# One decode step of two attention and SwiGLU layers: q in wider slices, accumulators opened by one matmul, x added by five matmuls

## The chip, the cores and the metric

The kernel runs on one core of one Trainium2 chip. The metric is device time in microseconds (us). Before the change the median of three runs is 528.95 us (528.78 to 529.55).

A core has five engines that run beside each other: TensorE (PE, with its weight loads listed apart as PEld), VectorE (DVE), ScalarE (ACT), GpSimd (POOL) and SyncE (SP). Sixteen DMA engines move data between HBM and the on-chip memory (SBUF); matmuls write to PSUM.

## The reference

One token `x` of 640 numbers goes twice through attention and a gated feed-forward net, with the same weights and the same cache both times:

```
x = x + A(layernorm(x));  x = x + B(layernorm(x));  x = x + A(layernorm(x));  x = x + B(layernorm(x))

A(x): q = x @ wq            # wq [640, 32*192]
      k, v = the last W = 4096 rows of each of 32 heads' caches, [4096, 192] each
      p = softmax(q k^T / sqrt(192));   return concat(p v) @ wo      # wo [32*192, 640]
B(x): return (silu(x @ w1) * (x @ w3)) @ w2     # w1, w3 [640, 1536], w2 [1536, 640]
```

All is bf16. Each head's k and v window is 1.5 MB, so one pass over wq, all k, all v, wo, w1, w3 and w2 is some 120 MB; what the second layer can reuse is limited by what fits into SBUF.

## The kernel before

**Pages.** `arena` is an SBUF tile of 16 slots (`NSLOT`), each of 6144 bf16 columns by 128 partitions (1.5 MB). Everything big arrives as a page of this size: five pages of wq (`("q", layer, c)`), one k and one v page per head, wo in pages `("o", layer, 0..4)` of nine chunks each (a chunk is 128 rows of wo, 640 columns), and w1, w3, w2 as `fa`, `fb`, `fc`, `fd`. The list `loads` (L158 to L191) holds all transfers in their order. `refill` (L193) issues the next one on SP's queue as soon as a slot is free; `done(key)` frees a slot after its last use. So transfers are in program order on one queue, and an issue waits for the instruction that last read the slot. Thirteen k pages of layer 0 stay in their slots for layer 1 (`RETAIN`; a fourteenth, `STASH`, is kept in PSUM and a side tile), which leaves about three slots free around the change of layers.

Two small tiles are loaded once, in layer 0, and used in both layers: `wo5`, the last three chunks of wo in layer 0's order, and `keep`, the last three chunks of w2. The heads are taken in groups of eight, in the order `ORDER = ((3, 2, 1, 0), (1, 0, 2, 3))`. The three chunks that wo5 holds come from group 0, the last of layer 0; in layer 1 the same tile is multiplied where the last three chunks of group 3 stand.

**The stages of a layer.** `layernorm` (L222) makes `xs`. `qproj` (L247) multiplies x with the five wq pages: per page 16 matmuls of 384 columns, four side by side in the PE array (`tile_position=(0, 32 * j)`), into one PSUM tile `q_ps`; ACT copies it to SBUF (L260), twelve small matmuls turn it (L262 to L267), DVE copies the turned q to `qt_sb` (L268). `build_w` (L270) places q of four heads as weights `wst` for the scores. Then `attention` runs over the heads: DVE transposes each k page (L293), PE multiplies it (`s_ps`), softmax follows in blocks of four heads, and the v pages are multiplied six heads later (`o_ps`). `combine` writes the result as columns of `otd`.

`wo_proj` (L392) multiplies otd with wo. Each product has one row, so four are set side by side in rows 0, 32, 64 and 96 of the accumulators `y_ps`, one for each half of the 640 columns. `y_open` (L383) first opens these accumulators: it multiplies a tile of zeros (`zero`, 128 x 32) with 320 columns, four times per accumulator, so that all rows hold 0. `y_to_residual` sums the four rows and adds them to the residual x, which stays in fp32 in `xsq[:, 0:5]`.

`ffn` (L412) multiplies with w1 and w3 (`g_ps`, `u_ps`), turns both with six small matmuls, and forms `htd` on ACT and DVE (L440 to L449). In layer 0 the product with w2 goes through y_open and y_to_residual as above. In layer 1 `last_rows` (L466) forms the output: four zero matmuls open `f_ps`, 20 fp32 matmuls add x (one column of xsq as weights, 32 columns of the 128 x 128 identity `ident` as data), and 48 products with w2 follow; DVE copies the rows (L482) and SP writes them out (L484). POOL builds `ident` in a free slot at the start of layer 1's ffn (L417, L418).

All engine instructions keep the order in which the code records them (`pin`). Every matmul is recorded in the helper `mm`, so the profile puts all of them on L80 and they are told apart by the tiles they write.

Of the kernel before, what the change touches and what calls it, by code (L numbers as in the profile page):

```python
# [41 lines left out]
def _ap(t, p0, npart, off, dims):  # L42
    ps = t.ap[0][0]
    return bass.AP(t.tensor, t.offset + p0 * ps + off, [[ps, npart]] + [list(d) for d in dims])
# [3 lines left out]
def kernel(  # L48
# [26 lines left out]
    def pin(ins):  # L75
        tc.keep_in_program_order(ins)
        return ins

    def mm(*a, **k):
        return pin(nc.tensor.matmul(*a, **k))  # L80
# [17 lines left out]
    nc.gpsimd.memset(sel4[:], 0.0)  # L98
    nc.gpsimd.affine_select(out=sel4[:], in_=sel4[:], compare_op=ALU.not_equal, fill=1.0, base=0,
                            pattern=[[-32, 4]], channel_multiplier=1)  # L100
    sel16 = cst.tile([P, 4, 4], BF16, name="sel16")
    nc.gpsimd.memset(sel16[:], 0.0)
    nc.gpsimd.affine_select(out=sel16[:], in_=sel16[:], compare_op=ALU.not_equal, fill=1.0, base=0,
                            pattern=[[-32, 4], [-1, 4]], channel_multiplier=1)


    sel = cst.tile([P, 2, HB, 16], BF16, name="sel")
# [20 lines left out]
    ptm = cst.tile([P, 16 * PW], BF16, name="ptm")  # L128
    otd = cst.tile([P, 48], BF16, name="otd")
    htd = cst.tile([P, 12], BF16, name="htd")  # L130
    zero = cst.tile([P, 32], BF16, name="zero")
    nc.gpsimd.memset(zero[:], 0.0)
    w20 = cst.tile([P, 768], BF16, name="w20")
    qt_sb = cst.tile([P, 2, 6, 16], BF16, name="qt_sb")
    rl = cst.tile([P, 1], F32, name="rl")


# [17 lines left out]
    def head(layer, g):  # L155
        return HG * ORDER[layer][g // HG] + g % HG

    for layer in range(2):  # L158
        for c in range(NCH):
            loads.append((("q", layer, c), [(0, PGW, wq_v[c])]))  # L160
        for i in range(H + LEAD):
            for kind, g, cache in (("v", i - LEAD, A_v_cache), ("k", i, A_k_cache)):
                if not 0 <= g < H:
                    continue
                h = head(layer, g)
                if kind == "k" and layer == 1 and h in RETAIN:
                    if h == STASH:
                        loads.append((("k", 1, h), []))
                    continue
                loads.append(((kind, layer, h),  # L170
                              [(0, PGW, cache[0, h, S0:SK, :].rearrange("(p t) d -> p (t d)", p=P))]))
        for w in range(6):
            parts, ci, end = [], 9 * w, min(9 * w + 9, 48)
            while ci < end:
                to = min(end, ci - ci % 12 + 12)
                parts.append((640 * (ci - 9 * w), 640 * (to - ci),
                              wo_v[ORDER[layer][ci // 12]][:, 640 * (ci % 12):640 * (ci % 12 + to - ci)]))
                ci = to
            if w < 5:
                loads.append((("o", layer, w), parts))  # L180
            elif layer == 0:
                assert len(parts) == 1 and parts[0][1] == 1920
                loads.append((None, [(wo5[:], parts[0][2])]))
        loads.append((("fa", layer), [(0, PGW, w1_v[:, 0:PGW])]))
        loads.append((("fb", layer), [(0, PGW, w3_v[:, 0:PGW])]))
        loads.append((("fc", layer), [(0, 1536, w1_v[:, PGW:]), (1536, 1536, w3_v[:, PGW:]),
                                      (3072, 2560, w2_v[:, 0:2560])]))
        fd = [(0, 3200)] if layer == 0 else [(0, 1280), (1280, 1280), (2560, 640)]
        loads.append((("fd", layer), [(o, n, w2_v[:, 2560 + o:2560 + o + n]) for o, n in fd]))
        if layer == 0:  # L190
            loads.append((None, [(keep[:], w2_v[:, 5760:7680])]))  # L191
# [55 lines left out]
    def qproj(layer):  # L247
        q_ps = ps_a.tile([P, 512], F32, tag="a", name="q_ps")
        for c in range(NCH):
            pg = page(("q", layer, c))  # L250
            for c2 in range(4):
                for j in range(4):
                    hp = 4 * j + c2
                    mm(q_ps[32 * j:32 * j + 32, 0:384], lhsT=xs[:, c, 3 - c2:35 - c2],
                       rhs=pg[:, 384 * hp:384 * hp + 384],
                       start=(c == 0 and c2 == 0), stop=(c == NCH - 1 and c2 == 3),
                       tile_position=(0, 32 * j))
            done(("q", layer, c))
        q_sb = w20
        pin(nc.scalar.copy(out=q_sb[:, 0:384], in_=q_ps[:, 0:384]))  # L260
        qt_ps = m_ps[0:32].rearrange("p (h i c) -> p h i c", h=2, i=6)
        for hh in range(2):  # L262
            for it in range(6):
                be, par = divmod(it, 2)
                o = 64 * (3 * hh + be) + par
                mm(qt_ps[:, hh, it, :], lhsT=q_sb[:, o:o + 63:2],
                   rhs=sel16[:].rearrange("p j c -> p (j c)"), start=True, stop=True)  # L267
        pin(nc.vector.tensor_copy(out=qt_sb[0:32], in_=qt_ps[:]))  # L268

    def build_w(b, first):  # L270
        engs = (nc.gpsimd, nc.scalar) + ((nc.vector, nc.vector) if first else (nc.gpsimd, nc.scalar))
        for a in range(4):
            dst = _ap(wst[:], 32 * a, 32, 8 * a + HB - 1, [[382, HB // 2], [191, 2], [32, 6]])
            src = _ap(qt_sb[:], 0 if first else 32 * a, 32, HB // 2 * b, [[1, HB // 2], [96, 2], [16, 6]])
            pin((engs[a].copy if engs[a] is nc.scalar else engs[a].tensor_copy)(out=dst, in_=src))  # L275
        if first:
            for a in range(1, 4):
                pin(nc.vector.tensor_copy(out=qt_sb[32 * a:32 * a + 32], in_=qt_sb[0:32]))
# [104 lines left out]
    def y_open(name):  # L383

        y_ps = [ps_a.tile([P, 512], F32, tag="a", name=f"{name}{i}") for i in range(2)]
        for nh in range(2):
            for j in range(4):
                mm(y_ps[nh][32 * j:32 * j + 32, 0:320], lhsT=zero[:], rhs=ptm[:, 0:320],
                   start=True, stop=False, tile_position=(0, 32 * j))
        return y_ps  # L390

    def wo_proj(layer):  # L392
        y_ps = y_open("y_ps")
        for w in range(6):
            pg = page(("o", layer, w)) if w < 5 else wo5
            for cc in range(min(9, 48 - 9 * w)):
                ci = 9 * w + cc
                j = ci % 4
                for nh in range(2):
                    mm(y_ps[nh][32 * j:32 * j + 1, 0:320], lhsT=otd[:, ci:ci + 1],  # L400
                       rhs=pg[:, 640 * cc + 320 * nh:640 * cc + 320 * nh + 320],
                       start=False, stop=(ci >= 44), tile_position=(0, 32 * j))
            if w < 5:
                done(("o", layer, w))
        y_to_residual(y_ps)
# [6 lines left out]
    def ffn(layer):  # L412
        if layer == 1:
            assert not loads
            spare = free[0] * PGW
            ident = arena[:, spare:spare + 256].bitcast(F32)
            nc.gpsimd.memset(ident, 0.0)  # L417
            nc.gpsimd.affine_select(out=ident, in_=ident, compare_op=ALU.not_equal, fill=1.0, base=0,  # L418
                                    pattern=[[-1, P]], channel_multiplier=1)
        g_ps = ps_a.tile([P, 512], F32, tag="a", name="g_ps")  # L420
        u_ps = ps_a.tile([P, 512], F32, tag="a", name="u_ps")
        for ps, kind, c0, c1, off in ((g_ps, "fa", 0, 4, 0), (u_ps, "fb", 0, 4, 0),
# [42 lines left out]

    def last_rows(ident):  # L466
        f_ps = ps_a.tile([P, 512], F32, tag="a", name="f_ps")
        for j in range(4):
            mm(f_ps[32 * j:32 * j + 32, 0:160], lhsT=zero[:], rhs=ptm[:, 0:160], start=True, stop=False,
               tile_position=(0, 32 * j))  # L470
        for c in range(NCH):
            for j in range(4):
                mm(f_ps[32 * j:32 * j + 1, c:160:NCH], lhsT=xsq[:, c:c + 1], rhs=ident[:, 32 * j:32 * j + 32],
                   start=False, stop=False, tile_position=(0, 32 * j))
        for fcx in (0, 1, 2, 3, 9, 10, 11, 4, 5, 6, 7, 8):
            pg, off = w2_chunk(1, fcx)
            for j in range(4):
                mm(f_ps[32 * j:32 * j + 1, 0:160], lhsT=htd[:, fcx:fcx + 1],
                   rhs=pg[:, off + 160 * j:off + 160 * j + 160],
                   start=False, stop=(fcx == 8), tile_position=(0, 32 * j))  # L480
        row = w20[:, 0:160]
        pin(nc.vector.tensor_copy(out=row, in_=f_ps[:, 0:160]))  # L482
        ps = row.ap[0][0]
        nc.sync.dma_start(out=out[0, 0, :].rearrange("(j i) -> j i", j=4),  # L484
                          in_=bass.AP(row.tensor, row.offset, [[32 * ps, 4], [1, 160]]))
# [69 lines left out]
```

## Time and profile before

| what | value |
| --- | --- |
| median of 3 runs | 528.95 us (528.78 to 529.55) |
| the profiled execution | span 527.8 us; its time around the span is not listed apart |
| read from HBM | 221.58 MB, 420 GB/s over the span |
| PE matmuls | 2487 in 275.8 us (52%) |
| PE weight loads | 2487 in 113.9 us (22%) |
| DVE | 393 instructions in 256.5 us (49%) |
| ACT | 192 in 62.3 us (12%) |
| POOL | 66 in 14.3 us (3%) |
| mean granted TensorE clock | 0.716 |

The span runs from the first to the last instruction of the program. A busy share is an average over stages with different limits, so a stage is read from its own window. "Idle before, <-releaser" is the time that an engine had nothing to do before an instruction, and what ended it. The granted clock is the share of TensorE's clock that it was given. An fp32 matmul shows as two weight loads and two matmuls in the trace, called passes here.

### The profile page before, as it was taken

The page shows a single profiled execution, that of the slowest core. Times are in us where ns is not written, and L with a number is a line of the kernel's source. Part 1 is how long each engine was busy: PE and PEld are TensorE (multiplying, and loading weights), DVE is VectorE, ACT ScalarE, POOL GpSimd, SP SyncE. Part 2 cuts the span into 40 slices and gives each one's busy share as a digit, 9 for nine tenths or more (in the row PEclk, how much of TensorE's full clock was granted, in tenths as well). Part 3 has the DMA queues.
Part 4 walks back from the last instruction along what each step waited for, and adds up shares of the span by engine and source line. Part 5 has one row for each costly group of instructions (what it writes and reads, how often), then busy time and mean ns, then how long its engine had stood idle before and what let it go on. Part 6 is the DMA issues. An engine that isn't in the chain of part 4 may idle for free.

```text
span 527.8 us, 6132 instructions
## 1 busy us (share of the span) xinstructions
PE 275.8 (52%) x2487; PEld 113.9 (22%) x2487; DVE 256.5 (49%) x393; ACT 62.3 (12%) x192; POOL 14.3 (3%) x66
## 2 busy tenths in 40 slices
PE   2354644463645555455445446678254655446545
PEld 1111212121212221122112212233121322112212
DVE  1199676656656475754001139431475654753001
ACT  1002020111102020102000002022111120202000
POOL 4000000000000000000000000000000000000000
PEclk9997968676766776586556557888677886586556
DMA  8999999999999999999999999999999999999995
GB/s 350 430 429 429 428 431 429 427 431 429 427 431 431 430 425 432 430 426 425 416 433 422 430 430 401 431 431 427 430 429 427 429 430 431 430 428 428 424 432 215
DMA packets 22356, 221.97 MB, mean 421 GB/s; under 512 B 2617, under 2 KB 2745, under 8 KB 5177
## 3 DMA queue, kind: packets, MB, share of 16 engines
q1 hardware_dynamic: 22184, 221.59, 99.1%
q8 instruction: 19, 0.31, 0.2%
q14 instruction: 9, 0.07, 0.0%
q10 hardware_dynamic: 144, 0.00, 0.0%
HBM read 221.58 MB, written 0.00 MB: 420 GB/s over the span
## 4 chain that ended last, share of the span: by engine, by line
DMA 86%; PE 6%; DVE 5%; ACT 1%; issue 1%; SPq 0%; DVEq 0%; ACTq 0%
DMA arena<-in_A_k_cache_dram 54%; DMA arena<-in_A_v_cache_dram 14%; DMA arena<-in_A_wo_dram 8%; DMA arena<-in_A_wq_dram 6%; DMA arena<-in_B_w_dram 5%; DVE arena L293 4%; PE s_ps L80 3%; PE o_ps L80 2%; PE y_ps L80 1%; SPq L203 0%; ACT w L330 0%; PE pss L80 0%; PE q_ps L80 0%; DVE t L315 0%; PE g_ps L80 0%
## 5 line engine op out<-in xcount | busy, mean ns | idle before, releaser
L80 PE MATMUL s_ps<-arena,wst 128*32 128x512 bf16 x768 | 155.2, 518 | 172.7 <-DVE arena L293 86.4
L293 DVE STREAM_TRANSPOSE arena<-arena 128x1536 uint32<-128x1536 uint32 x100 | 171.2, 1754 | 77.3 <-DMA arena<-in_A_k_cache_dram 77.0
L80 PE MATMUL o_ps<-arena,ptm 128*8 128x384 bf16 (+1 forms) x1024 | 116.7, 425 | 11.4 <-DMA arena<-in_A_v_cache_dram 11.3
L80 PEld LDWEIGHTS <-wst 128*32 128x32 bf16 x768 | 52.9, 115 | 257.9 <-issue 226.7
L80 PEld LDWEIGHTS <-ptm 128*8 128x8 bf16 (+1 forms) x1024 | 41.0, 100 | 49.0 <-issue 38.8
L325 ACT ACTIVATE tb<-m 32x16 f32<-32x16 f32 x16 | 3.4, 215 | 280.6 <-DVE m L322 280.6
L343 ACT COPY ptm<-w 32x64 bf16<-32x64 bf16 x80 | 23.6, 295 | 44.5 <-PE o_ps L80 41.4
L80 PE MATMUL y_ps<-arena,otd 128*1 128x320 bf16 x180 | 16.5, 448 | 15.0 <-DMA arena<-in_A_wo_dram 15.0
L80 PE MATMUL q_ps<-arena,xs 128*32 128x384 bf16 x160 | 14.5, 519 | 17.5 <-DMA arena<-in_A_wq_dram 14.9
L376 DVE SCALAR_TENSOR_TENSOR w<-pss,rl,mask 64x192 bf16<-64x192 f32 x16 | 6.7, 416 | 31.7 <-PE pss L80 31.7
L275 POOL COPY wst<-qt_sb 32x24 bf16<-32x24 bf16 x30 | 8.4, 281 | 434.4 <-PE s_ps L80 315.8
L333 DVE STREAM_TRANSPOSE w<-w 64x512 bf16<-64x512 bf16 x16 | 11.3, 705 | 14.4 <-ACT w L330 14.4
L241 DVE CAST w<-y_ps 128x320 bf16<-128x320 f32 x3 | 1.5, 492 | 33.8 <-PE y_ps L80 33.8
L315 DVE TENSOR_REDUCE t<-s_ps 64x1 f32<-64x512 f32 x16 | 10.6, 663 | 12.2 <-PE s_ps L80 12.1
L80 PEld LDWEIGHTS <-xs 128*32 128x32 bf16 x240 | 8.8, 125 | 35.1 <-issue 23.0
L268 DVE CAST qt_sb<-pss 32x192 bf16<-32x192 f32 x2 | 0.7, 345 | 30.9 <-PE pss L80 30.9
L343 DVE COPY ptm<-w 32x64 bf16<-32x64 bf16 x48 | 10.0, 208 | 11.7 <-PE o_ps L80 10.4
L348 DVE RECIPROCAL rl<-pss 64x1 f32<-64x1 f32 x16 | 2.6, 165 | 20.5 <-PE pss L80 20.4
L80 PEld LDWEIGHTS <-otd 128*1 128x1 bf16 x192 | 6.4, 102 | 25.2 <-issue 21.1
L330 ACT ACTIVATE w<-s_ps,nbt 64x512 bf16<-64x512 f32 x16 | 10.9, 682 | 5.6 <-DVE nbt L327 5.6
L369 ACT CAST w<-o_ps 128x384 bf16<-128x384 f32 x16 | 7.7, 478 | 31.7 <-PE o_ps L80 23.3
L80 PE MATMUL pss<-w,sel 128*64 128x192 bf16 x32 | 6.0, 273 | 9.5 <-ACT w L369 6.4
(81 smaller groups left out, 107.8 us busy)
## 6 DMA issues: line engine op xcount, KB each, us to landing
arena<-in_A_v_cache_dram SPq DMA_DIRECT2D x64, 1536.0 KB, 29.2
arena<-in_A_k_cache_dram SPq DMA_DIRECT2D x50, 1536.0 KB, 29.2
arena<-in_A_wq_dram SPq DMA_DIRECT2D x10, 1536.0 KB, 9.5
arena<-in_A_wo_dram SPq DMA_DIRECT2D x6, 1440.0 KB, 20.8
arena<-in_B_w_dram SPq DMA_DIRECT2D x4, 1536.0 KB, 10.9
arena<-in_A_wo_dram SPq DMA_DIRECT2D x4, 960.0 KB, 16.5
arena<-in_A_wo_dram SPq DMA_DIRECT2D x4, 480.0 KB, 15.0
arena<-in_B_w_dram SPq DMA_DIRECT2D x4, 384.0 KB, 14.8
```

The source lines that it names most:

```text
L80: return pin(nc.tensor.matmul(*a, **k))
L241: pin(nc.vector.tensor_copy(out=y_sb[:, 320:640], in_=y_ps[1][:, 0:320]))
L275: pin((engs[a].copy if engs[a] is nc.scalar else engs[a].tensor_copy)(out=dst, in_=src))
L293: pin(nc.vector.transpose(x[:, w * sp:w * (sp + 1)].bitcast(U32), x[:, w * sp:w * (sp + 1)].bitcast(U32)))
L315: pin(nc.vector.reduce_max(out=t0[:, 0:1], in_=s_ps[0:64, :], axis=AX.X))
L325: pin(nc.scalar.mul(out=tb[32:64, :].rearrange("p (a z) -> p a z", a=4)[:, :, 0:HB], in_=mb, mul=-SCALE))
L330: pin(nc.scalar.activation(out=e[:], in_=s_ps[0:64, :], func=ACTF.Exp, bias=nbt[:, 0:1], scale=SCALE, accum_out=l[:]))
L333: pin(nc.vector.transpose(et[:], e[:]))
L343: pin((eng.copy if eng is nc.scalar else eng.tensor_copy)(out=dst, in_=src))
L348: pin(nc.vector.reciprocal(out=rl[half], in_=rl_ps[half]))
L369: pin(nc.scalar.copy(out=o_sb[:, 0:384], in_=o_ps[:, 0:384]))
L376: pin(nc.vector.scalar_tensor_tensor(out=om, in0=ot_ps[half], scalar=rl[half], in1=mask[half].unsqueeze(2).broadcast_to([64, 16, 12]), op0 ...
```

## The change

Four edits are made together.

- **q.** wq's 6144 columns are taken as 12 slices of 512 instead of 16 of 384. A page now takes 12 matmuls, three after each other in each of the four column groups. The turn takes 16 matmuls of 12 columns instead of 12 of 16, and writes PSUM with a step of 16 elements; `qt_sb` now has one row of six per head, and build_w reads it contiguously.
- **Opening.** `zero` is one column, broadcast to 128, and one matmul opens a whole accumulator; y_open issues two instead of eight.
- **Kept chunks.** `wo_order` puts the three chunks of group 3 last in both layers, so wo5 holds what both layers multiply last. In layer 0 this changes the order in which wo's chunks are loaded and multiplied; in layer 1 the order stays.
- **x in the last product.** f_ps is not opened by zeros. POOL builds an identity of 32 columns repeated over four groups of partitions (`ident`, now a pair) and `xw`, 640 fp32 columns in which each group of 32 partitions holds x in one column per chunk. Five fp32 matmuls with 128 columns of xw as weights add x to all four rows at once, and the first of them opens f_ps.

```
-    zero = cst.tile([P, 32], BF16, name="zero")
+    zero = cst.tile([P, 1], BF16, name="zero")
...
+    def wo_order(layer):
+        last = ORDER[1][3]
+        kept = [12 * ORDER[layer].index(last) + e for e in (9, 10, 11)]
+        return [ci for ci in range(48) if ci not in kept] + kept
...
-            for c2 in range(4):
+            for c2 in range(3):
                 for j in range(4):
-                    hp = 4 * j + c2
-                    mm(q_ps[32 * j:32 * j + 32, 0:384], lhsT=xs[:, c, 3 - c2:35 - c2],
-                       rhs=pg[:, 384 * hp:384 * hp + 384],
+                    sl = 3 * j + c2
+                    mm(q_ps[32 * j:32 * j + 32, 0:512], lhsT=xs[:, c, 3 - c2:35 - c2],
+                       rhs=pg[:, 512 * sl:512 * sl + 512],
...
-        pin(nc.scalar.copy(out=q_sb[:, 0:384], in_=q_ps[:, 0:384]))
-        qt_ps = m_ps[0:32].rearrange("p (h i c) -> p h i c", h=2, i=6)
-        for hh in range(2):
-            for it in range(6):
-                be, par = divmod(it, 2)
-                o = 64 * (3 * hh + be) + par
-                mm(qt_ps[:, hh, it, :], lhsT=q_sb[:, o:o + 63:2],
-                   rhs=sel16[:].rearrange("p j c -> p (j c)"), start=True, stop=True)
+        pin(nc.scalar.copy(out=q_sb[:, 0:512], in_=q_ps[:, 0:512]))
+        qt_ps = m_ps[0:32].rearrange("p (s n) -> p s n", s=12)
+        for blk in range(8):
+            for par in range(2):
+                o = 64 * blk + par
+                mm(qt_ps[:, :, 2 * blk + par], lhsT=q_sb[:, o:o + 63:2],
+                   rhs=sel12[:].rearrange("p j c -> p (j c)"), start=True, stop=True)
...
         for nh in range(2):
-            for j in range(4):
-                mm(y_ps[nh][32 * j:32 * j + 32, 0:320], lhsT=zero[:], rhs=ptm[:, 0:320],
-                   start=True, stop=False, tile_position=(0, 32 * j))
+            mm(y_ps[nh][:, 0:320], lhsT=zero[:].broadcast_to([P, P]), rhs=ptm[:, 0:320], start=True, stop=False)
...
-            ident = arena[:, spare:spare + 256].bitcast(F32)
+            ident = arena[:, spare:spare + 64].bitcast(F32)
             nc.gpsimd.memset(ident, 0.0)
-            nc.gpsimd.affine_select(out=ident, in_=ident, compare_op=ALU.not_equal, fill=1.0, base=0,
-                                    pattern=[[-1, P]], channel_multiplier=1)
+            for j in range(4):
+                nc.gpsimd.affine_select(out=ident, in_=ident, compare_op=ALU.not_equal, fill=1.0, base=-32 * j,
+                                        pattern=[[-1, 32]], channel_multiplier=1)
+            xw = arena[:, spare + 64:spare + 64 + 1280].bitcast(F32)
+            nc.gpsimd.memset(xw, 0.0)
+            for j in range(4):
+                nc.gpsimd.tensor_copy(out=xw[32 * j:32 * j + 32, 32 * j:640:128], in_=xsq[32 * j:32 * j + 32, 0:NCH])
+            ident = (ident, xw)
...
-        for j in range(4):
-            mm(f_ps[32 * j:32 * j + 32, 0:160], lhsT=zero[:], rhs=ptm[:, 0:160], start=True, stop=False,
-               tile_position=(0, 32 * j))
+        eye, xw = ident
         for c in range(NCH):
-            for j in range(4):
-                mm(f_ps[32 * j:32 * j + 1, c:160:NCH], lhsT=xsq[:, c:c + 1], rhs=ident[:, 32 * j:32 * j + 32],
-                   start=False, stop=False, tile_position=(0, 32 * j))
+            mm(f_ps[:, c:160:NCH], lhsT=xw[:, 128 * c:128 * c + 128], rhs=eye, start=(c == 0), stop=False)
```

## The prediction

> **What bounds the kernel now.** I read the page first, then the chain, then the stages by window, and last the timeline of the closing microseconds.
>
> ```profile
> span 527.8 us, 6132 instructions
> PE 275.8 (52%) x2487; PEld 113.9 (22%) x2487; DVE 256.5 (49%) x393; ACT 62.3 (12%) x192; POOL 14.3 (3%) x66
> DMA  8999999999999999999999999999999999999995
> q1 hardware_dynamic: 22184, 221.59, 99.1%
> q8 instruction: 19, 0.31, 0.2%
> DMA 86%; PE 6%; DVE 5%; ACT 1%; issue 1%; SPq 0%; DVEq 0%; ACTq 0%
> ```
>
> The data queue holds the 16 DMA engines for 99.1% of the span, and 86% of the chain is DMA. No engine is busy for more than 52%. Work on PE, ACT, DVE or POOL therefore counts only where it holds back an issue until the queue runs dry, or where it lies behind the last landing. The second queue, q8, brings instructions: 19 packets, 0.31 MB, so 16 KB each.
>
> The columns of the next view are the stretch, its length, busy time with a count for PE, PEld, DVE, ACT and POOL, the granted clock, the DMA share and GB/s.
>
> ```profile
> 300.00:310.00 10.00, 4.01 (x48) 1.81 (x47) 0.00 (x0) 0.00 (x0) 0.00 (x0) 0.50 1.01 429
> 310.00:320.00 10.00, 6.79 (x45) 2.43 (x38) 8.19 (x10) 0.77 (x2) 0.28 (x1) 0.50 1.01 428
> 521.50:522.00 0.50, 0.50 (x35) 0.48 (x38) 0.11 (x1) 0.18 (x1) 0.00 (x0) 0.57 0.46 179
> 522.00:522.50 0.50, 0.27 (x32) 0.14 (x19) 0.43 (x4) 0.00 (x0) 0.00 (x0) 1.00 0.36 128
> 523.00:523.40 0.40, 0.40 (x32) 0.40 (x28) 0.00 (x0) 0.00 (x0) 0.00 (x0) 1.00 0.11 29
> 523.40:524.00 0.60, 0.27 (x16) 0.12 (x5) 0.00 (x0) 0.00 (x0) 0.00 (x0) 1.00 0.05 13
> ```
>
> At the second layer's q (300 to 320 us) DMA stays full. At the end it tapers: 0.11 of 16 engines is under two engines, and 0.05 over 0.6 us is 0.5 us of one engine. So a single engine carries data from about 523.4 to 523.9 while the rest is done. The clock goes from 0.50 to 1.00 at about 521.9.
>
> ```profile
> 514.33 0.60 PE L80 MATMUL pss<-xsq,onesD 128*128 128x12 f32 x2 [0.45 <-DVE xsq L223]
> 521.57 0.33 PE L80 MATMUL f_ps<-ptm,zero 128*32 128x160 bf16 x4
> 521.68 0.60 PE L80 MATMUL f_ps<-arena,xsq 128*1 128x32 f32 x40
> 522.64 0.19 DVE L449 TENSOR_TENSOR htd<-gut,ex 128x12 bf16<-128x12 f32 x1
> 522.88 0.45 PE L80 MATMUL f_ps<-arena,htd 128*1 128x160 bf16 x16 [0.61 <-DVE htd L449]
> ...
> 524.08 0.56 PE L80 MATMUL f_ps<-arena,htd 128*1 128x160 bf16 x12 [0.41 <-DMA arena<-in_B_w_dram]
> 524.08 0.15 PEld L80 LDWEIGHTS <-htd 128*1 128x1 bf16 x8 [0.56 <-issue]
> 524.40 0.09 PEld L80 LDWEIGHTS <-htd 128*1 128x1 bf16 x3 [0.17 <-issue]
> 524.70 0.32 DVE L482 CAST w<-f_ps 128x160 bf16<-128x160 f32 x1 [1.87 <-PE f_ps L80]
> 525.08 0.66 SPq L484 DMA_DIRECT2D out_dram<-w  x1
> ```
>
> x's matmuls end at 522.28, 0.6 us before htd lets the products start. PE then waits 0.41 us for w2, and the last four products start at 524.40, on the last 160 KB. Then come the cast and the write. Only these last pieces are bare.
>
> **The change part by part.** I sum against the profiled span of 527.8. The listed median, 528.95, is 1.15 above it; I hold that difference fixed.
>
> *q.* Per page 16 matmuls of 384 columns become 12 of 512, four side by side: 4 x 384 and 3 x 512 are both 1536 columns, so the 1.47 us per page stays, and the page is freed when it was. Behind them the ACT copy (0.478 us at 384 columns, 0.425 at 320 in the y copy, so 0.83 ns a column) grows by 128 x 0.83 = 0.11 us. The transposes (12 in 0.49 us, each 0.17 alone, so 0.03 apart) become 16, +0.12 us; strided PSUM writes could make it +0.16 (all by count), and nothing excludes that narrower ones keep the 0.49 (+0). build_w's copies move the same 24 elements. So q is ready 0.1 to 0.3 us later, I take 0.23, once per layer. What hides it: DMA at 1.01 in the windows above. Its queue holds two or three pages of 3.65 us there; a page freed 0.23 us later joins a queue with over 3 us left. If that cover were gone it would cost 0.23 per layer.
>
> *Opened accumulators.* Eight zero matmuls in 0.72 us become two. In both wo products PE then still waits 0.2 us for the first wo page, and in the first layer's w2 for htd; gain 0. PE would only wait longer for the same landing.
>
> *Kept wo chunks.* Layer 0 loads the same seven pieces with the same bytes, in another order of sizes (5760, 5760, 1920, 3840, 3840, 1920, 5760 columns in place of 5760, 1920, 3840, 3840, 1920, 5760, 5760), and multiplies in that order. Nothing is added to SP. Cost 0.
>
> *POOL.* Two instructions (0.21 and 0.29 us at 477.7) become ten. Memsets, five-column copies and 32-column selects lie by the nearest rows at 0.2 to 0.3 us, the 640-column memset at most five times 0.21. Six of them, under 2.5 us, run at 478; nothing is behind them on POOL. The four copies wait for xsq (DVE, 514.08) and end near 515.3, and the matmuls want them at 521.5. Cost 0. If they slowed DVE's layernorm beside them, PE's 0.47 us wait for w3's page takes it up.
>
> *x joins.* Four zero matmuls and 40 one-column passes become ten passes (five fp32 matmuls, two each) that load 128 fp32 columns. Nearest row: layernorm's pair, also 128 fp32 columns. Two passes of 0.378 cover 0.60, so they start 0.22 apart at clock 0.50; I take 0.23 for 32 columns instead of 12. Bounds: 0.19 (the two loads, 0.310 each, cover 0.50) and 0.31 (no overlap). Ten passes are 2.3 us (1.9 to 3.1) at half clock. They start at about 521.55. Until 521.93 1.65 passes run, the other 8.35 at full clock take 8.35 x 0.115 = 0.96: they end at 522.89, and htd lets the products start at 522.88. Cost 0, but with no slack: the 0.6 us of idle are used up.
>
> By the Trainium skill, "TensorE: Matmul & The Clock Gate", section LDWEIGHTS, a weight load takes its columns / 1.2 in ns, and fast weight load is not for fp32. By that, ten loads are an estimated 1.07 us and x would end at 522.6, with 0.25 to spare; layernorm's pair is slower here and is what I use.
>
> *Instructions.* PE executes 2487 + 2487 = 4974. Counted on the built programs, 168 go: 32 per layer in q, 12 per opened pair (three), and 68 in the last product. 19 packets over 4974 is one per 262. The last packet came in the tail: the window 521.9 to 524.1 has one q8 packet at 2.6% of 16 engines x 2.2 us = 0.92 us, with 115 PE instructions still to run. 168 later is past the program's end or among the last products, after the data has landed. The engine that carried it is the one still alone after 523.4: without it, data ends 0 to 0.92 us earlier. The other engine working in 523.0 to 523.4 ends near 523.4, so I take 0.5. The last four products start at 523.9 in place of 524.40; the 44 before them are through by then (36 cover 522.88 to 523.67, 0.231 each, so they start 0.016 apart, and 44 from 522.88 start by 523.57). Gain 0.5.
>
> Sum: -0.5, a span of 527.3, a time of 528.45.
>
> **The rivals.**
> - *x's passes hold the products back (slower).* If PE is still at half clock, x ends at 521.55 + 2.3 = 523.85 (3.1: 524.65). The 48 products, 0.98 us at full and about 1.8 at half clock, end at 525.65 (526.45) in place of 524.63: 529.95 (530.75). It decides from x longer than 2.1 us, since 524.63 - 0.98 - 521.55 = 2.1. For it: the clock rises only 0.4 us after x begins, and may rise later in another execution. Against: PE has been at work since 516.25 with two short gaps, and in layer 0's ffn the clock rose after the same work (0.90 in the window 286 to 288).
>   The Trainium skill's "TensorE: Matmul & The Clock Gate" says (The HAM clock gate) that the window in which PE's activity is judged is free-running, so the moment of the rise would differ from run to run; one trace cannot show that.
> - *The fetch was covered.* The last landing is then as late as before and the time is 528.95. For it: other engines also taper to 523.4, and the packet is small. The Trainium skill's "Runtime: NRT & Kernel Launch", section Instruction fetch mechanics, calls the cost of a 16 KiB refill mostly hidden, which would give this time; this trace has a refill in the taper, where little covers it.
> - *More is gained (faster).* The whole 0.92 us comes off, and another of the 18 remaining packets falls where it costs less. The window 252 to 254, which holds one at 253.6, moved 371 GB/s in place of 430, so it lost 2 x 59 / 430 = 0.27 us. With both, 528.95 - 0.92 - 0.27 = 527.76.
> - *q is on the path.* Layer 1's 0.23 us shows in full: with the gain 528.7, without it 529.2.
>
> **How the numbers follow.** 0.2% of 528.95 is 1.06 us, about what a measurement of this kernel can tell from no change. My forecast (528.45) has 0.42, the covered fetch 0.18, q on the path 0.08: all are within 0.2%. More gained has 0.15, faster. x holding the products back has 0.17; by its end at 530.75 it is slower, near its beginning it is within, so 0.14 slower and 0.03 within. That gives faster 0.15, same 0.71, slower 0.14. The range runs from 527.7 (the whole fetch and a little more) to 530.1 (half clock at my price): about 0.1 lies beyond each end.
>
> **What would show it.** Right: one q8 packet fewer before the last landing, the last products starting near 523.9, f_ps<-arena x10 ending by 523.0, DMA windows full at 300 to 330. Wrong: PE's htd products start later than 523.6, or right after x's passes with no wait for htd; or the last landing stays at 524.4. A queue that empties in 300 to 330 would say that q counts.

## The result and the profile after

The changed kernel takes **535.04 us** (median of four runs, 534.82 to 535.22); the kernel before, run beside it, takes 528.87 (528.75 to 529.55). The ratio is 1.0113, 95% interval 1.0100 to 1.0126: 6.2 us slower, where 528.45 and "within 0.2%" were predicted, and above the whole range. The profiled execution has a span of 533.2 us and a time of 535.06.

These lines of the page of the kernel after answer to those shown of before; the row GB/s has one number for each of 40 slices of the span.

```profile
span 533.2 us, 5978 instructions
PE 283.3 (53%) x2403; PEld 114.6 (21%) x2403; DVE 256.3 (48%) x393; ACT 62.5 (12%) x192; POOL 16.1 (3%) x74
DMA  8999999999999999999999999999999999999995
GB/s 352 427 425 422 423 424 424 426 425 424 422 425 423 425 427 423 422 426 424 416 424 415 414 425 417 423 425 425 423 423 421 428 425 426 423 422 423 420 426 218
q1 hardware_dynamic: 22184, 221.59, 99.2%
```

The row GB/s of the kernel before:

```profile
GB/s 350 430 429 429 428 431 429 427 431 429 427 431 431 430 425 432 430 426 425 416 433 422 430 430 401 431 431 427 430 429 427 429 430 431 430 428 428 424 432 215
```

The data queue moves the same 22184 packets and 221.59 MB and is as full as before. Only it is full for longer: 99.2% of 533.2 us is 528.9 us, where 99.1% of 527.8 were 523.1. So 5.8 us lie in the transfers themselves, and no engine and no wait need be asked for them. The row GB/s says where: nearly everywhere; it is lower than before in 34 of the 40 slices.

The same stretches by window, first of the kernel before, then after (the last two columns are DMA share and GB/s):

```profile
90.00:120.00 30.00, 15.41 (x117) 6.11 (x117) 18.52 (x24) 3.53 (x11) 0.56 (x2) 0.70 1.01 429
180.00:210.00 30.00, 15.82 (x120) 6.32 (x121) 17.95 (x23) 3.53 (x11) 0.56 (x2) 0.68 1.01 429
```

```profile
90.00:120.00 30.00, 15.20 (x116) 6.04 (x116) 18.18 (x23) 3.52 (x11) 0.56 (x2) 0.70 1.01 425
180.00:210.00 30.00, 14.80 (x116) 5.96 (x116) 18.31 (x24) 3.53 (x11) 0.56 (x2) 0.72 1.01 424
300.00:310.00 10.00, 3.93 (x36) 1.40 (x36) 0.00 (x0) 0.00 (x0) 0.00 (x0) 0.50 1.00 413
310.00:320.00 10.00, 5.54 (x49) 1.93 (x41) 4.20 (x8) 0.88 (x2) 0.28 (x1) 0.53 1.01 424
```

At an equal share of 1.01 the engines move 424 or 425 GB/s in place of 429, in stretches of plain attention, which the four edits leave as they were but for what build_w's short copies read (on POOL 0.56 us in both). Ten microseconds hold fewer than three pages, so the two rows of layer 1's q (300 to 320 us) swing more, but their share is full. The packets of the trace show it too: those of 12288 bytes take 467.0 ns on average against 462.2.

The tail, lines of the timeline of the kernel after:

```profile
527.38 1.38 PE L80 MATMUL f_ps<-arena 128*128 128x32 f32 x10
528.52 0.19 DVE L460 TENSOR_TENSOR htd<-gut,ex 128x12 bf16<-128x12 f32 x1
528.76 0.45 PE L80 MATMUL f_ps<-arena,htd 128*1 128x160 bf16 x16
529.24 0.72 PE L80 MATMUL f_ps<-arena,htd 128*1 128x160 bf16 x20
530.02 0.32 DVE L489 CAST w<-f_ps 128x160 bf16<-128x160 f32 x1 [1.31 <-PE f_ps L80]
```

The tail runs in the forecast steps, only later: x's ten passes end at 528.76, when htd has just been written (528.71), and the 48 products run through without the wait for w2 that stood ahead of the last twelve.

So what slows every transfer? The one thing in the change that reaches all of them is an address. The small tiles are laid out ahead of `arena` in units of 32 bytes. `zero` had 32 bf16 columns, 64 bytes; one column takes one unit. In the built programs arena therefore starts at byte 24032 of each partition in place of 24064. 24064 is 94 x 256; 24032 is 224 bytes past a multiple of 256. Every page row is 12288 bytes, 48 x 256, so all 16 slots moved off together.

### The profile page after: what moved, and what is told of

Its sections match the earlier page's. It is cut to its first block, busy times and chain, and to the rows that moved or that the text cites. A ratio compares the mean times of both kernels' runs of the same rounds, so it can differ in the third digit from the quotient of the medians.

```text
span 533.2 us, 5978 instructions
## 1 busy us (share of the span) xinstructions
PE 283.3 (53%) x2403; PEld 114.6 (21%) x2403; DVE 256.3 (48%) x393; ACT 62.5 (12%) x192; POOL 16.1 (3%) x74
## 3 DMA queue, kind: packets, MB, share of 16 engines
q1 hardware_dynamic: 22184, 221.59, 99.2%
## 4 chain that ended last, share of the span: by engine, by line
DMA 84%; PE 8%; DVE 5%; ACT 1%; issue 1%; SPq 0%; DVEq 0%; ACTq 0%
DMA arena<-in_A_k_cache_dram 46%; DMA arena<-in_A_v_cache_dram 16%; DMA arena<-in_A_wo_dram 9%; DMA arena<-in_A_wq_dram 7%; DMA arena<-in_B_w_dram 6%; DVE arena L300 4%; PE s_ps L80 3%; PE o_ps L80 2%; PE y_ps L80 1%; PE q_ps L80 1%; PE u_ps L80 1%; PE f_ps L80 0%; SPq L210 0%; PE pss L80 0%; ACT w L337 0%
## 5 line engine op out<-in xcount | busy, mean ns | idle before, releaser
L80 PE MATMUL s_ps<-arena,wst 128*32 128x512 bf16 x768 | 160.5, 535 | 166.9 <-DVE arena L300 81.7
L80 PEld LDWEIGHTS <-wst 128*32 128x32 bf16 x768 | 54.6, 118 | 254.2 <-issue 226.3
L80 PE MATMUL q_ps<-arena,xs 128*32 128x512 bf16 x120 | 13.9, 600 | 18.4 <-DMA arena<-in_A_wq_dram 15.7
L80 PEld LDWEIGHTS <-xs 128*32 128x32 bf16 x200 | 6.9, 119 | 37.5 <-issue 27.5
```

## The experiments

**Theory:** the whole loss is the new start of the pages, and it is paid on each transfer. **Rivals:** the other edits slow the DMA (wider q, ten POOL instructions, another order of wo), or the longer queue is an effect of where the work lies in time. The kernel before was run beside each group: 529.12 us in the first two groups, 529.24 in the third.

### The pages back on their old addresses

The changed kernel with all four edits, `zero` 32 columns wide again, of which one is used:

```diff
-    zero = cst.tile([P, 1], BF16, name="zero")
+    zero = cst.tile([P, 32], BF16, name="zero")
...
-  lhsT=zero[:].broadcast_to([P, P])
+  lhsT=zero[:, 0:1].broadcast_to([P, P])
```

> The changed kernel with one tile put back to its old size: zero is again 128 x 32 (its first column is broadcast), so that arena starts at byte 24064 of each partition as in the kernel before, and not at 24032. All the changed instructions stay. Theory A (the smaller zero tile moved arena off a 512-byte boundary, and every page lands 1% slower for it): 528.2 to 529.0 us, the 12288-byte packets back at a rate of 429 GB/s in the saturated windows. Theory B (the time came from the changed instructions, or from where the instruction packets fall): 534.5 to 535.5 us and 424 GB/s.

Measured: **528.57 us** (528.19 to 529.47), 0.9989 of before (0.9977 to 1.0000), span 527.0, packets of 12288 bytes 462.5 ns. Nothing but the width of that tile, and with it 32 bytes of address, lies between this kernel and the changed one, which is 6.5 us slower. Two windows and the tail of its timeline:

```profile
90.00:120.00 30.00, 15.17 (x117) 6.08 (x117) 18.52 (x24) 3.52 (x11) 0.56 (x2) 0.70 1.01 429
180.00:210.00 30.00, 16.02 (x120) 6.37 (x121) 18.09 (x23) 3.53 (x11) 0.56 (x2) 0.67 1.01 430
```

```profile
521.26 1.27 PE L80 MATMUL f_ps<-arena 128*128 128x32 f32 x10
522.39 0.19 DVE L460 TENSOR_TENSOR htd<-gut,ex 128x12 bf16<-128x12 f32 x1
522.63 0.45 PE L80 MATMUL f_ps<-arena,htd 128*1 128x160 bf16 x16
523.12 0.63 PE L80 MATMUL f_ps<-arena,htd 128*1 128x160 bf16 x20
523.80 0.32 DVE L489 CAST w<-f_ps 128x160 bf16<-128x160 f32 x1 [1.22 <-PE f_ps L80]
```

The queue is back at 429 and 430 GB/s with every edit in place, and the cast of the result starts at 523.80, where before had 524.70.

### The address alone

The kernel before, with nothing but the small tile's width changed (its matmuls read the same zeros, by broadcast or from the first 32 columns):

```diff
-    zero = cst.tile([P, 32], BF16, name="zero")
+    zero = cst.tile([P, 1], BF16, name="zero")     # arena at 24032
+    zero = cst.tile([P, 48], BF16, name="zero")    # or 24096
+    zero = cst.tile([P, 96], BF16, name="zero")    # or 24192
+    zero = cst.tile([P, 64], BF16, name="zero")    # or 24128
```

> The kernel before with only the zero tile narrowed to one column (broadcast to 32 in the matmuls), so arena starts at 24032. Nothing else of the change is in it. Theory A: 534 to 535.5 us, 424 GB/s in the saturated windows. Theory B: 528.9 us, 429 GB/s.

> The kernel before with the zero tile 32 bytes longer: arena starts at 24096, 32 bytes past a 512-byte boundary where the changed kernel's is 32 bytes short of one. Theory A with a fixed price for any start off the boundary (one more piece per packet, 49 in place of 48): 534 to 535.5 us. Theory A with a price by distance above the boundary: 529.5 to 530.5 us. By the Trainium skill, DMA: Bandwidth & Descriptors, section How a descriptor splits into AXI transactions, a start 32 bytes past a 256-byte boundary costs one beat of 32 bytes in 384 and one 224 bytes past it seven: an estimate of 0.3% here and 1.8% in the changed kernel. Theory B: 528.9 us.

> The kernel before with the zero tile 128 bytes longer: arena starts at 24192, on a 64-byte and a 128-byte boundary but not on a 256-byte one. Theory A with a 64-byte grid: 528.9 us. Theory A with a grid of 256 bytes or more and a fixed price: 534 to 535.5 us; with a price by distance: about 533 us. Theory B: 528.9 us.

> The kernel before with the zero tile 64 bytes longer: arena starts at 24128, on a 64-byte boundary but not on a 128-byte one. If 64 bytes is the grid: 528.9 us. If the grid is 256 bytes or more with a near fixed price, 534 to 535.5 us, between the 535.1 of +32 and the 534.2 of +128.

One row of the windows of each, in this order of starts: 24032, 24096, 24192, 24128.

```profile
180.00:210.00 30.00, 15.49 (x116) 6.25 (x116) 18.28 (x24) 3.53 (x11) 0.56 (x2) 0.66 1.01 424
```

```profile
180.00:210.00 30.00, 15.56 (x116) 6.27 (x116) 18.29 (x24) 3.54 (x11) 0.56 (x2) 0.65 1.01 424
```

```profile
180.00:210.00 30.00, 15.14 (x117) 6.15 (x117) 18.38 (x24) 3.53 (x11) 0.56 (x2) 0.71 1.01 426
```

```profile
180.00:210.00 30.00, 15.80 (x117) 6.26 (x117) 18.33 (x23) 3.53 (x11) 0.56 (x2) 0.66 1.01 426
```

The kernel before, moved by one tile's width and otherwise as it was, loses what the changed kernel lost, and it does so to both sides: 32 bytes up costs as 32 bytes down. The times stand in the table below.

### Which grid

24064 is a multiple of 512 as well. Here arena goes down by 256, to 23808, an odd multiple of 256: five small tiles of the kernel before take the place of others that are not in use at the time, and `zero` has one column.

```diff
-    zero = cst.tile([P, 32], BF16, name="zero")
+    zero = cst.tile([P, 1], BF16, name="zero")
...
-        ex = sml.tile([P, 12], F32, tag="ex", name="ex")
+        ex = sml.tile([P, 12], F32, tag="t1", name="ex")     # likewise ut, gut, nv and l
```

> The kernel before with 256 bytes taken out of the small tiles ahead of arena (zero one column wide; nv, l, ex, ut and gut share the room of other small tiles): arena starts at 23808, an odd multiple of 256. If 256 bytes is the grid: 528.5 to 529.3 us and 429 GB/s in the saturated windows. If 512 bytes is the grid: 532 to 535.5 us. The shared small tiles lie in no long stretch of waits and should cost nothing that can be seen.

Measured: 529.12 us, 0.9999 of before (0.9990 to 1.0008), and 429 and 430 GB/s. 256 bytes are enough.

| arena starts at | past a multiple of 256 | us | ratio to before (95%) | mean of a 12288-byte packet |
| --- | --- | --- | --- | --- |
| 24064 (before) | 0 | 529.12 | 1 | 462.2 ns |
| 23808 | 0 | 529.12 | 0.9999 (0.9990 to 1.0008) | 462.3 |
| 24096 | 32 | 535.11 | 1.0119 (1.0104 to 1.0134) | 467.2 |
| 24128 | 64 | 534.76 | 1.0102 (1.0088 to 1.0116) | 466.1 |
| 24192 | 128 | 534.17 | 1.0104 (1.0087 to 1.0121) | 465.5 |
| 24032 | 224 | 535.87 | 1.0128 (1.0112 to 1.0143) | 467.6 |

By the packets, 16384 of them on 16 engines, 24032 costs 1024 x (467.6 - 462.2) ns = 5.5 us, most of the 6.75 us by which it is slower; the shorter packets make up part of the rest.

The Trainium skill, "DMA: Bandwidth & Descriptors", section "How a descriptor splits into AXI transactions", says that a descriptor is cut into pieces that must start on 256-byte addresses, and that a start past one costs the 32-byte beats in between. The grid agrees with the runs, though the section speaks of what a transaction reads, and here the address that moved is the one written to. The price does not agree: an aligned row of 12288 bytes is 384 beats, and by the section's count a start 32, 64, 128 or 224 bytes past makes it 385, 386, 388 or 391, an estimated 0.3, 0.5, 1.0 and 1.8%. The packets grew by 1.1, 0.8, 0.7 and 1.2%: being off the grid costs, and the price does not grow with the distance. By the packets the two starts on a multiple of 64 bytes cost somewhat less than the two that are not.

### Half of the pages

If it is paid per transfer, half of the pages off the grid pay about half. Arena has 16 columns more, and slots 8 to 15, which take 45% of the bytes, start 32 bytes later:

```diff
-    arena = arn.tile([P, NSLOT * PGW], BF16, name="arena")
+    arena = arn.tile([P, NSLOT * PGW + 16], BF16, name="arena")
...
+    def slot(s):
+        return s * PGW + (16 if s in range(8, 16) else 0)
```

> The kernel before with arena where it was (24064) and slots 8 to 15 of it moved 32 bytes up, so that part of the pages start off the boundary. Counted over the transfers, 45% of the bytes land in these slots. If the price is paid per page that starts off the boundary: 528.9 + 0.45 x 6.1 = 531.7 us (531.2 to 532.2). If it is the base of the tile that counts: 528.9.

Measured: 531.23 us, 1.0033 (1.0020 to 1.0046). Two windows:

```profile
90.00:120.00 30.00, 15.05 (x116) 6.50 (x116) 18.26 (x23) 3.53 (x11) 0.56 (x2) 0.70 1.01 426
180.00:210.00 30.00, 16.31 (x116) 6.47 (x116) 18.46 (x23) 3.54 (x11) 0.56 (x2) 0.66 1.01 428
```

It lies between, which is against a cause outside the transfers. It is at the low end of what was expected: 45% of the 1.19% at 32 bytes would be 0.54%, outside the interval.

The trace shows why it is less. It is of an execution of 530.42 us, and its 12288-byte packets average 463.2 ns, 1.0 above before, where 45% of the 5.0 at 24096 would be 2.3. In order of their start, 128 of these packets make a page, and the first 16 pages fill slots 0 to 15 in turn. The pages in slots 8, 9 and 10 are off the grid, and yet their packets average 460.0 to 460.3 ns, as on the grid; the page in slot 11 has 463.1, those in slots 12 to 15 have 465.4 to 465.6 (one has 470.5, where before has 464.1), and the next one, on the grid again in slot 0, has 460.8. The kernels with all pages off the grid begin in the same way: at 24032 (the changed kernel and the kernel before) and at 24096 the second to fourth page average 460.0 to 461.6 ns, the sixth to tenth 465.0 to 469.7 (in before 460.0 to 463.9). So the theory is right about the address, but the price is not paid by every transfer off the grid: it sets in with about the fourth or fifth such page in a row. In layer 1 pages on and off the grid are mixed here, and few runs are that long. Why the price sets in late is open.

### The tail: the instruction packet and x

What is left of the change without the address is some 0.5 us of gain. The prediction put it down to the 16 KB instruction packet that ran in the tail. The aligned kernel shows that packet after the data, at 523.7, but it also has fewer instructions in all. So 168 PE instructions were put back, as 84 matmuls of one column ahead of the first layernorm, first in the aligned kernel, then in the kernel before; and x was joined in the old way in the aligned kernel.

```diff
     def attention(layer):
+        if layer == 0:
+            for _ in range(84):
+                mm(m_ps[0:1, 0:1], lhsT=onesb[:], rhs=onesb[:], start=True, stop=True)
         layernorm()
```

> The changed kernel with zero as wide as before (the aligned one), and 84 matmuls of one column, with their weight loads, ahead of the first layernorm, where PE waits for x: 168 PE instructions, as many as the change took away; their results are not used. If the last instruction packet makes the last landing late, as the prediction has it, this brings it back into the tail: the last landing 0.5 to 0.9 us later than in the aligned kernel, 529.0 to 529.4 us where that one takes 528.5. If the packet is harmless: no later landing, and the time of the aligned kernel.

> The kernel before with 84 one-column matmuls (168 PE instructions) ahead of the first layernorm and nothing else changed, so the same instruction boundary is passed some 6 us earlier in the tail. Theory (the last instruction packet, while it shares the taper with w2's last pieces, holds back the last landing): no instruction packet between 519 and 523.5, the last landing 0.6 to 0.7 us earlier than before's 524.36 (near 523.7), the last four products right behind the 44 before them, the cast near 524.0, a time 0.3 to 0.8 under the kernel before: 528.3 to 528.8. Rival (the packet is hidden, what moved the tail in the aligned kernels is the new order of x or of wo): the last landing stays at 524.3 to 524.4 and the time within 0.2 of before: 528.9 to 529.3.

The old join (four zero matmuls and 20 small fp32 ones on the 128 x 128 identity) in the aligned kernel:

```diff
-            mm(f_ps[:, c:160:NCH], lhsT=xw[:, 128 * c:128 * c + 128], rhs=eye, start=(c == 0), stop=False)
+            for j in range(4):
+                mm(f_ps[32 * j:32 * j + 1, c:160:NCH], lhsT=xsq[:, c:c + 1], rhs=ident[:, 32 * j:32 * j + 32],
+                   start=False, stop=False, tile_position=(0, 32 * j))
```

> The changed kernel with the pages back on their old addresses and x joined in the old way (four zero matmuls, 20 small fp32 matmuls), the other three edits kept. Theory (x's new matmuls end when htd is ready and cost nothing): the same time as the aligned kernel with the new x join, 528.57, within 0.3 (528.3 to 528.9); the products start after htd in both, with about 0.6 us of idle PE ahead of them here. Rival (the new x join saves or costs something of its own, by the fewer instructions or the pages that POOL writes): over 0.3 us away from 528.57 to one side. The 68 PE instructions that come back put the last instruction packet some 70 instructions before the end, among the last products; if it held the last landing there, the time would be 0.3 to 0.6 longer.

Measured, with the last instruction packet and w2's last transfer as the profiles have them:

| kernel | us | ratio to before (95%) | last packet of q8 | last w2 piece: issue to landing |
| --- | --- | --- | --- | --- |
| before | 529.12 and 529.24 | 1 | 522.01 to 522.93 | 511.00 to 524.36: 13.36 |
| aligned | 528.57 | 0.9989 (0.9977 to 1.0000) | from 523.67 | 510.76 to 523.46: 12.70 |
| aligned, 168 more | 528.76 | 0.9993 (0.9985 to 1.0002) | 518.1 | 510.75 to 523.45: 12.70 |
| before, 168 more | 528.90 | 0.9988 (0.9977 to 0.9999) | 522.29 to 523.25 | 510.58 to 523.24: 12.66 |
| aligned, old x | 528.89 | 0.9986 (0.9975 to 0.9996) | 522.93 to 523.82 | 511.29 to 523.90: 12.61 |

The 168 in the aligned kernel were expected to bring the packet back into the tail and the landing with it. They put it at 518.1, where the queue is still full, and the landing did not move, so this run does not decide about a packet in the taper.

The kernel before with 168 idle instructions at its start gains about as much as the aligned kernel, so a gain of this size needs none of the four edits. It is at the edge of what the runs can tell: the upper ends of the intervals lie between 0.9996 and 1.0002. And what was expected of this kernel is only half borne out: a packet still ran in its tail, and yet the last landing came early. The windows of before with 168 more, from 523.00 on, answer to the last two that the prediction shows of before:

```profile
523.00:523.40 0.40, 0.40 (x24) 0.26 (x12) 0.00 (x0) 0.00 (x0) 0.00 (x0) 1.00 0.00 0
523.40:524.00 0.60, 0.12 (x4) 0.00 (x0) 0.32 (x1) 0.00 (x0) 0.00 (x0) 1.00 0.00 0
```

No data moves there, where before had 29 and 13 GB/s. In before the packet began 11.01 us after the last issue, and right behind its end a row of 1280-byte data packets ran one after another until 523.94. With 168 more it began 11.71 us after the last issue; data ended at 522.95, 0.3 us ahead of the packet's own end. By these two traces a packet in the taper would cost only if data is still queued behind it. The trace does not name the engine of a packet, so that the row of data was on the packet's engine is read from the times, not shown.

The kernel at 23808 speaks against it. It has as many instructions as before, and its last packet too ran in the taper, from 521.57 to 522.52, 10.80 us after the last issue, with data moving until 523.20. Two steps of its chain:

```profile
510.77 12.88 DMA arena<-in_B_w_dram
523.69 0.27 PE f_ps L80 x4
```

The last landing came 12.88 us after its issue, half a microsecond sooner than in before, and the last four products start at 523.69 in place of 524.40; still the kernel takes 529.12 us, as before does. So a packet with data behind it is not enough for a late landing, and a landing that is earlier in one execution is not a shorter time in the median. What held the last landing back in the kept execution of before is open.

And x: the old join leaves PE idle for 0.7 us ahead of the products, the new one for 0.1 us (x's passes end at 522.53, the products start at 522.63), at the same time within the intervals.

```profile
521.84 0.51 PE L80 MATMUL f_ps<-arena,xsq 128*1 128x32 f32 x40
523.08 0.45 PE L80 MATMUL f_ps<-arena,htd 128*1 128x160 bf16 x16 [0.72 <-DVE htd L454]
```

## Why the prediction was wrong

- **What bounds the kernel** was right: DMA throughout. That is what made the missed step expensive, since a loss in the transfers has nothing to hide behind.
- **The step that failed** is "Opened accumulators". It counted matmuls: "Eight zero matmuls in 0.72 us become two ... gain 0. PE would only wait longer for the same landing." The matmuls are free, as said. But the same edit cuts `zero` from 64 bytes to 2, and with it moves arena and every page in it. The landing was not the same. This term, 0 in the sum, is +6.5 us (535.04 less 528.57); the transfers became slower, 467.0 ns for a 12288-byte packet in place of 462.2. The kernel before with only this tile changed shows +6.75. No rival had it: 0.14 for slower was all x's.
- **Could it have been seen?** The trace of before has no page off the grid, so it had no row for the price. It could be seen that something moves: the sizes in the diff and the units of 32 bytes give the new start of arena. The price had no bound, and the range said nothing of it.
- **q:** right. The queue stays full at 310 to 320 us (1.01), and with the pages on the grid all edits together take no longer than the kernel before.
- **Kept chunks, POOL:** right as far as the sum shows. POOL went from 14.3 to 16.1 us with eight instructions more. The aligned kernel (0.9989) and the kernel before with 168 more (0.9988) leave nothing over some 0.15% for all edits together. Neither was tried alone.
- **x:** right, in place and nearly in size. Ten passes were to last from 521.55 to 522.89, 1.34 us, and end when htd is there. They last 1.38 us in the changed kernel, and 1.27 at full clock in the aligned one (0.127 each, 0.115 predicted), and end 0.05 us behind htd and 0.05 ahead of it. The slack is used up and nothing is lost. Products right behind x's passes, with no wait for htd, had been named as a sign of being wrong; the changed kernel shows them, and they cost nothing, since htd had been written only 0.05 us before. The rival of half clock did not come: the clock is at 1.00 from 527.6 in the changed kernel, 0.2 us after x begins, and from 518.5 in the aligned one. That moment moves by over 3 us between the aligned kernel and before, so the rival was not an empty one.
- **Instructions:** the size came close, but the runs do not show its reason. A gain of 0.5 to a time of 528.45 was forecast, and the aligned kernel has 528.57, a gain of 0.55 with an interval that ends at 0. Its last landing is 0.90 us earlier in the profile, of which 0.24 is an earlier issue and 0.66 a shorter way. But "168 later is past the program's end or among the last products" is only one of the ways to this: two kernels with a packet still in the tail gained the same by the ratio, and the kernel at 23808, with a landing only 0.2 to 0.3 us slower than theirs, gained nothing. So that the size came close is at least in part luck.

## What to carry to other kernels

When the bound is DMA, read a diff for bytes of SBUF too: each tile that grows, shrinks or goes moves every tile laid out behind it, and the big ones' start, modulo 256, belongs in the sum beside the instructions. If a kernel becomes slower by about 1% with the data queue equally full, compare GB/s in stretches that the change does not touch, before any engine is looked at. Give the pages a start of their own on a multiple of 256 bytes, so that no small tile decides it; here the version that does so, 528.57 us, has all four edits and is no slower than the kernel before.

## What was not expected of the hardware

- With all SBUF rows of 12288 bytes starting off a multiple of 256 bytes the kernel takes 1.0 to 1.3% longer (534.2 to 535.9 us against 529.1), 32 bytes off about as much as 128 or 224; an odd multiple of 256 costs nothing (529.12). The price is not there from the first such page: the first few in a row take 460 to 462 ns a packet, and from about the fifth on it is some 465 (at 32 or 224 bytes past).
- The last instruction packet, 16 KB, takes 0.89 to 0.96 us in the five traces with the pages on the grid in which it began before the data had ended (0.92 in before). Whether it holds back the last landing is not settled: from issue to landing it took 13.36 us in before and 12.88 at 23808, both with data behind the packet, and 12.61 to 12.70 in four other kernels.
